# Routing attention and PReLU feed-forward: the keys' cluster masks four slots later on ScalarE, the range checks on inverted denominators

## The chip, the cores and the metric

The kernel runs on one core of one Trainium2 chip. The metric is the device time of one execution in microseconds; a comparison uses the median of several. The engines are named as the profile names them: PE is TensorE (PEld its weight loads), ACT is ScalarE, DVE is VectorE, POOL is GpSimd, SP is SyncE, which only issues transfers here. "L384" is line 384 of the kernel.

## The reference, cut to what matters

```python
# q, k, v: (4, 8, 768, 64), centroids: (8, 16, 64)
q_assign = argmax(einsum('bhsd,hcd->bhsc', q_n, c_n), -1)   # nearest of 16 clusters
k_assign = argmax(einsum('bhsd,hcd->bhsc', k_n, c_n), -1)
mask = q_assign[:, :, :, None] == k_assign[:, :, None, :]
scores = where(mask, q @ k^T / 8, -1e9)
attn = softmax(scores)                                       # minus the row's maximum
x = (attn @ v), heads joined: (3072, 512)
h = x @ w_in                                                 # w_in: (512, 2048), float64
g = maximum(h, 0) + alpha * minimum(h, 0)
out = g @ w_out                                              # w_out: (2048, 512), float64
```

The kernel leaves the row's maximum out of the softmax. So it checks that every denominator lay in a safe range, and has a general path behind one branch at its end for inputs where one did not.

## The kernel before

Work goes by pairs of heads (16 of them: 4 batches by 4), each in two halves of 384 queries, each half in three steps of two key chunks of 128. Pairs 0 to 3 (n < NCH) have their masks added to the scores by a small matmul; later pairs multiply the exponentials by the mask on VectorE. While the first pairs run, 32 tiles of float64 weights are fetched and turned into float32 in four stages: a fetch, a split on VectorE, a scaling on ScalarE, a joining on VectorE that ends with a multiplication on GpSimd.

A step has five slots. `tick` begins one and runs the pieces that `later` put off to it. Each engine executes its instructions in the order in which the program has them.

```python
ps_s = tile_pool(name="ps_s", bufs=2, space=PS)     # scores, two banks each
ps_v = tile_pool(name="ps_v", bufs=1, space=PS)     # product with v
ps_m = tile_pool(name="ps_m", bufs=1, space=PS)     # similarities, row sums and others
ps_f = tile_pool(name="ps_f", bufs=2, space=PS)     # feed-forward

def later(slots, piece):
    due.setdefault(now[0] + slots, []).append(piece)

def tick():
    now[0] += 1
    for piece in due.pop(now[0], []):
        piece()

# conversion of one weight tile, POOL's part last
def split():                                        # L241, L243, DVE
    nc.vector.tensor_scalar(out=power, in0=hi, scalar1=0x7FF00000, ...)
    nc.vector.tensor_scalar(out=dst.bitcast(U32), in0=hi, scalar1=0x000FFFFF, ...)
def scale():                                        # L247, L249, ACT
    nc.scalar.activation(out=power, in_=power, func=AF.Relu, ...)
    nc.scalar.activation(out=dst, in_=dst.bitcast(U32), func=AF.Identity, ...)
def join():                                         # L253, L256, DVE; L259, POOL
    nc.vector.scalar_tensor_tensor(out=power, in0=hi, ..., in1=power, ...)
    nc.vector.scalar_tensor_tensor(out=dst, in0=lo, ..., in1=dst, ...)
    nc.gpsimd.tensor_tensor(out=dst, in0=dst, in1=power.bitcast(FP32), op=ALU.mult)

def check(n, half, dens):                           # L310, two reductions
    i = 2 * n + half
    for to, op in ((lowest, ALU.min), (highest, ALU.max)):
        nc.vector.tensor_reduce(out=to[:, i:i + 1], in_=dens.bitcast(I32), axis=AX.X, op=op)

def prep_features(n, g):      # n < NCH: transposes L324 (PE), copies L328 (ACT) one slot later

def prep_sims(n):             # three steps ahead of pair n (n < NCH)
    ps = misc()
    ...                       # L351: similarities to the clusters, 8 matmuls
    later(1, lambda: prep_argmax(n, ps))

def prep_argmax(n, ps):
    ...                       # L359 to L377: argmax as one-hot rows, all DVE
    if n >= NCH:
        return                # (ahead of L377)
    member = fsp.tile([P, 2, HS], BF16, name="member")
    nc.vector.transpose(out=member[:, 0, :], in_=top...)          # L381
    for h in (1, 0):                                              # L384
        nc.scalar.activation(
            out=member[HP:P, h, :], in_=member[HP:P, 0, :], func=AF.Identity,
            scale=pick[HP:P, h:h + 1], bias=pick[HP:P, h + 2:h + 3])
    members[n] = member

def prep_queries(n, half, h): # L423, n < NCH: SP copies the query rows of member (partitions 0 to 63)

def score(n, half, chunks):
    ...                       # L463: scores; L473: adds the mask from member (n < NCH)
    ...                       # L484: exponentials, ACT, PSUM to SBUF

def invert(n, half):          # pairs 4 to 15: sums came by L530
    ps = totals.pop((n, half))
    inv = rdp.tile([P, 2 * NX], FP32, name="inv")
    nc.vector.reciprocal(out=inv, in_=ps[:, 0:2 * NX])            # L540
    check(n, half, ps[:, 0:2 * NX])
    ...                       # L545: two transposes spread inv into rd
    rds[n, half] = rd

def weigh(m, denominators=False):
    ...                       # L566: denominators by matmul (the early passes)
    ...                       # L573: product with v
    if denominators and done:
        ...                   # L579: transpose of the denominators out of PSUM
        check(n, half, denT[:, 0:NX // 2, 0])
        ...                   # L586, L590: reciprocals and copies to inv
        ...                   # L593: transpose to rd

def normalise(n, half):       # L600: xT = product * rd, DVE

# feed-forward of one half batch, in pieces between the steps:
#   hidden(f): L623 (PE), L630 and L631 (ACT), L615 (DVE); final(...): L643 (PE), L649 or L651

# one step of the first part:
tick(); score(step)
tick(); invert(prior); weigh(previous exponentials); mask, normalise(prior), add_up ...
for i in range(3):
    tick(); feed(...); prepare(...)      # prep_sims(n) in the first of these slots
    convert_next()                       # from step 1 on
```

The passes of pairs 0 to 3 in their first half are steps 0 to 11; their denominators come by L566. `invert` and L530 serve the 28 other passes.

Of the kernel before, what the change touches and what calls it, by code (L numbers as in the profile page):

```python
# [12 lines left out]
I32 = mybir.dt.int32  # L13
AF = mybir.ActivationFunctionType
ALU = mybir.AluOpType
AX = mybir.AxisListType
PS = bass.MemoryType.PSUM
P = 128
# [3 lines left out]
def kernel(  # L22
# [11 lines left out]
    nc = tc.nc  # L34
# [55 lines left out]
    def later(slots, piece):  # L90
        due.setdefault(now[0] + slots, []).append(piece)
# [57 lines left out]
    for g in range(P // Q):  # L149
        r = slice(g * Q, (g + 1) * Q)  # L150
        nc.gpsimd.tensor_copy(
            out=fold[r, :].rearrange("p (a i) -> p a i", i=Q),
            in_=ident[r, None, r].broadcast_to((Q, P // Q, Q)))
# [10 lines left out]
    pick = const.tile([P, 4], FP32, name="pick")  # L164
    for h in range(2):
        nc.vector.tensor_reduce(
            out=pick[:, h:h + 1],
            in_=fold.rearrange("p (a h c) -> p a h c", h=2, c=NC)[:, 0, h, :],
            axis=AX.X, op=ALU.add)
# [130 lines left out]

    lowest = const.tile([P, 2 * NP], FP32, name="lowest")
    highest = const.tile([P, 2 * NP], FP32, name="highest")
    WORDS = [float((127 + e) * 2 ** 23) for e in (-40, 50)]

    def check(n, half, dens):
        i = 2 * n + half
        for to, op in ((lowest, ALU.min), (highest, ALU.max)):
            nc.vector.tensor_reduce(out=to[:, i:i + 1], in_=dens.bitcast(I32), axis=AX.X,  # L310
                                    op=op)


# [28 lines left out]
    NX = GT * NG  # L342
    assert NB % NG == 0 and W == Q and GT == HJ and NX * Q == HS
    everys, keys, members = {}, {}, {}
    HP = P // 2

    def prep_sims(n):
        hp = pairs[n][1]
        ps = misc()
        for g in range(NG):  # L350
            nc.tensor.matmul(out=ps[g * W:(g + 1) * W, 0:HS],  # L351
                             lhsT=cT[:, hp * W:(hp + 1) * W],
                             rhs=qkTs[n][:, g * HS:(g + 1) * HS],
                             start=True, stop=True)
        later(1, lambda: prep_argmax(n, ps))

    def prep_argmax(n, ps):
        simT = asg.tile([P, HS], FP32, name="simT")
        nc.vector.transpose(out=simT, in_=ps[:, 0:HS])  # L359
        sim = simT.rearrange("p (t c) -> p t c", c=NC)  # L360


        mx = asg.tile([P, 2 * NX], FP32, name="mx")
        nc.vector.tensor_reduce(out=mx, in_=sim, axis=AX.X, op=ALU.max)
        top = asg.tile([P, 2 * NX, NC], BF16, name="top")
        nc.vector.tensor_tensor(
            out=top, in0=sim, in1=mx[:, :, None].broadcast_to((P, 2 * NX, NC)),
            op=ALU.is_ge)
        nc.vector.tensor_tensor(
            out=top, in0=top, in1=rank[:, None, :].broadcast_to((P, 2 * NX, NC)),  # L370
            op=ALU.mult)
        first = asg.tile([P, 2 * NX], BF16, name="first")
        nc.vector.tensor_reduce(out=first, in_=top, axis=AX.X, op=ALU.max)
        firsts[n] = first
        if n >= NCH:
            return
        nc.vector.tensor_tensor(  # L377
            out=top, in0=top, in1=first[:, :, None].broadcast_to((P, 2 * NX, NC)),
            op=ALU.is_equal)
        member = fsp.tile([P, 2, HS], BF16, name="member")  # L380
        nc.vector.transpose(out=member[:, 0, :], in_=top.rearrange("p t c -> p (t c)"))  # L381

        for h in (1, 0):
            nc.scalar.activation(  # L384
                out=member[HP:P, h, :], in_=member[HP:P, 0, :], func=AF.Identity,
                scale=pick[HP:P, h:h + 1], bias=pick[HP:P, h + 2:h + 3])
        members[n] = member

    def prep_clusters(n):


        first = firsts.pop(n)
        ps = misc()
        for g in range(NG):
            nc.tensor.matmul(out=ps[:, g * 2 * NX:(g + 1) * 2 * NX], lhsT=spread[:, g, :],
                             rhs=first, start=True, stop=True)
        every = fsp.tile([P, NG, GT, NG, 2], BF16, name="every")
        everys[n] = every
        later(1, lambda: nc.scalar.copy(every.rearrange("p g i r h -> p (g i r h)"),
                                        ps[:, 0:NG * 2 * NX]))  # L400
        later(2, lambda: prep_keys(n))
# [132 lines left out]
    def invert(n, half):  # L534

        if (n, half) not in totals:
            return
        ps = totals.pop((n, half))
        inv = rdp.tile([P, 2 * NX], FP32, name="inv")
        nc.vector.reciprocal(out=inv, in_=ps[:, 0:2 * NX])  # L540
        check(n, half, ps[:, 0:2 * NX])
        rd = rdp.tile([P, HS], FP32, name="rd")
        for h in range(2):
            r = slice(h * D, (h + 1) * D)
            nc.vector.transpose(  # L545
                out=rd[r, :],
                in_=inv[r, h * NX:(h + 1) * NX, None].broadcast_to((D, NX, Q)))
        rds[n, half] = rd

    def weigh(m, denominators=False):  # L550


        first = waiting[:m]
        del waiting[:m]
        n, half = first[0][:2]
        done = first[-1][2] == NJ - 1
        if (n, half) not in pos:
            pos[n, half] = ps_v.tile([P, 512], FP32, name="vps")
        po = pos[n, half]
        if denominators:  # L560

            for _, _, c, e in first:
                for h in range(2):
                    for x in range(2):
                        r = h * D + x * Q
                        nc.tensor.matmul(out=first_den[r:r + Q, 0:HS // 2],  # L566
                                         lhsT=ones[:, 0:Q],
                                         rhs=e[:, h, x * HS // 2:(x + 1) * HS // 2],
                                         start=(c == 0), stop=(c == NJ - 1))
        for _, _, c, e in first:  # L570
            for h in range(2):
                r = h * D
                nc.tensor.matmul(out=po[r:r + D, 0:HS], lhsT=vts[n][:, h, c, :],  # L573
                                 rhs=e[:, h, :], start=(c == 0), stop=(c == NJ - 1))
        if denominators and done:


            denT = asg.tile([P, NX, Q], FP32, name="simT")
            nc.vector.transpose(  # L579
                out=denT[:, 0:NX // 2, :].rearrange("p x i -> p (x i)"),  # L580
                in_=first_den[:, 0:HS // 2])
            check(n, half, denT[:, 0:NX // 2, 0])
            inv = rdp.tile([P, 2 * NX], FP32, name="inv")
            for g in range(P // Q):
                h, x = divmod(g, 2)
                nc.vector.reciprocal(  # L586
                    out=inv[h * D:h * D + Q, x * NX // 2:(x + 1) * NX // 2],
                    in_=denT[g * Q:(g + 1) * Q, 0:NX // 2, 0])
            for h in range(2):
                nc.vector.tensor_copy(out=inv[h * D + Q:(h + 1) * D, 0:NX],  # L590
                                      in_=inv[h * D:h * D + Q, 0:NX])
            rd = rdp.tile([P, HS], FP32, name="rd")
            nc.vector.transpose(out=rd, in_=inv[:, 0:NX, None].broadcast_to((P, NX, Q)))  # L593
            rds[n, half] = rd

    def normalise(n, half):
        b, hp = pairs[n]
        if (b, half) not in xTs:
            xTs[b, half] = xpool.tile([P, NCH, HS], FP32, name="xT")
        nc.vector.tensor_tensor(out=xTs[b, half][:, hp, :],  # L600
                                in0=pos.pop((n, half))[:, 0:HS],
                                in1=rds.pop((n, half)), op=ALU.mult)
# [114 lines left out]
    for u in range(-AHEAD, TOGETHER):  # L717
        for piece in load_at.get(u, []):
            piece()
        n, half, s = steps[max(u, 0)]  # L720
# [8 lines left out]
        if ended:  # L729
            invert(*prior[:2])  # L730
        if u > 0:
            weigh(GROUP, denominators=u <= UB)
# [33 lines left out]
    for u in range(TOGETHER, NS + 1):  # L766
        for piece in load_at.get(u, []):
            piece()
        if u < NS:
            n, half, s = steps[u]  # L770
        if s == 0 or u == NS:
# [3 lines left out]
            if u < NS:  # L775
                score(n, half, range(0, NJ // 2), alone=NJ // 2 - 1)
            tick()
            invert(*prior)
            weigh(GROUP if u == TOGETHER else NJ)
            if u < NS:  # L780
                for chunk in last(NJ // 2):
# [36 lines left out]
    while due:  # L818
# [3 lines left out]
    nc.vector.tensor_reduce(out=good[:, 1:2], in_=lowest, axis=AX.X, op=ALU.min)  # L822
    nc.vector.tensor_scalar(out=good[:, 0:1], in0=good[:, 0:1], scalar1=WORDS[1],
                            scalar2=None, op0=ALU.is_le)
    nc.vector.tensor_scalar(out=good[:, 1:2], in0=good[:, 1:2], scalar1=WORDS[0],
                            scalar2=good[:, 0:1], op0=ALU.is_ge, op1=ALU.mult)
# [163 lines left out]
```

## Time and profile before

| | |
|---|---|
| median of 3 runs | 1032.72 us (1032.67 to 1032.76) |
| span of the profiled execution | 1032.8 us |
| PE busy | 998.5 us, 97% |
| PEld busy | 490.1 us, 47% |
| DVE busy | 673.8 us, 65% |
| ACT busy | 325.0 us, 31% |
| POOL busy | 52.5 us, 5% |
| L384, masks on ACT | 8 instructions, 700 ns each, 14.6 to 68.0 us |
| L310, checks on DVE, pairs by L540 | 56 instructions, 168 and 121 ns each |
| L310, checks on DVE, beside L579 | 8 instructions, 163 and 152 ns each |
| ACT waited for L381 | 19.7 us in 4 times |
| PE's L351 waited for L310 | 4.1 us in 2 times |

Busy times are sums over the whole span. Their shares differ by stage: the first 97 us hold the early passes and most of the weights' conversion, then attention and feed-forward share TensorE, and the last 90 us are feed-forward alone. A line of waits reads: the waiting engine, tile and line, an arrow to what released it, the total in us, how many times, and the longest. Durations of neighbouring VectorE instructions can overlap in the trace, so the cost of a short one in a row is the distance between starts.

### The profile page before, as it was taken

What the parts mean: (1) busy time and instruction counts of PE and PEld (TensorE: products, weight loads), DVE (VectorE), ACT (ScalarE), POOL (GpSimd) and SP (SyncE); (2) the same over time, 40 slices, a digit from 0 to 9 for tenths busy, and PEclk for the clock granted to TensorE, in tenths of its full rate; (3) what the DMA queues carried; (4) which work ended last, traced back from release to release, by engine and by line L of the source; (5) the groups of instructions that cost most, each with busy time, mean ns of one, the idle gap of its engine ahead of it and who ended that gap; (6) DMA issues with size and microseconds to landing.
All of it is one profiled execution on the core that took longest, in us unless ns stands there. A gap on an engine that the chain in (4) does not pass through costs nothing.

```text
span 1032.8 us, 10335 instructions
## 1 busy us (share of the span) xinstructions
PE 998.5 (97%) x3923; PEld 490.1 (47%) x3923; DVE 673.8 (65%) x1183; ACT 325.0 (31%) x620; POOL 52.5 (5%) x71
## 2 busy tenths in 40 slices
PE   7789999899999999999999999999999999999997
PEld 4334444345454454545455454545545454544553
DVE  3688878868666576868856675878867675662111
ACT  3555545232232232313233141313324141321120
POOL 1132322200000000000000000000000000000000
PEclk8899999999999999999999999999999999999999
DMA  9343664121000230213000202304000000000000
GB/s 206 122 130 105 137 142 126 26 41 36 1 0 11 52 47 11 35 36 57 1 0 1 62 17 29 46 11 82 1 1 1 31 0 1 1 11 20 1 0 34
DMA packets 121705, 43.13 MB, mean 42 GB/s; under 512 B 113952, under 2 KB 114480, under 8 KB 121648
## 3 DMA queue, kind: packets, MB, share of 16 engines
q1 hardware_dynamic: 121472, 42.35, 18.7%
q8 instruction: 33, 0.54, 0.2%
q14 instruction: 24, 0.20, 0.1%
q10 hardware_dynamic: 176, 0.04, 0.0%
HBM read 35.69 MB, written 6.29 MB: 41 GB/s over the span
## 4 chain that ended last, share of the span: by engine, by line
PE 87%; DVE 8%; ACT 2%; issue 1%; POOL 1%; DVEq 0%; POOLq 0%
PE fps L623 31%; PE fps L643 30%; PE vps L573 11%; PE sps L463 9%; PE fps L463 3%; PE mps L351 1%; DVE power L253 1%; DVE acc L508 1%; PE sps L473 1%; DVE w_out_sb L243 1%; ACT member L384 1%; DVE w_in_sb L256 1%; DVE power L241 0%; PE fps L324 0%; DVE w_out_sb L256 0%
## 5 line engine op out<-in xcount | busy, mean ns | idle before, releaser
L623 PE MATMUL fps<-xT,w_in_sb 128*128 128x384 f32 x1024 | 342.6, 492 | 2.1 <-DVE xT L600 2.1
L643 PE MATMUL fps<-w_out_sb,gT 128*128 128x512 f32 x768 | 335.6, 594 | 0.9 <-DVE gT L615 0.9
L623 PEld LDWEIGHTS fps<-xT,w_in_sb 128*128 128x128 f32 x1024 | 192.1, 191 | 146.7 <-issue 7.8
L643 PEld LDWEIGHTS fps<-w_out_sb,gT 128*128 128x128 f32 x768 | 144.7, 190 | 177.8 <-issue 167.4
L615 DVE SCALAR_TENSOR_TENSOR gT<-neg,alpha_neg,gT 128x384 f32<-128x384 f32 x128 | 78.3, 613 | 132.7 <-ACT neg L631 131.3
L630 ACT ACTIVATE gT<-fps 128x384 f32<-128x384 f32 x128 | 62.7, 490 | 276.7 <-PE fps L623 276.7
L463 PE MATMUL sps<-qkT 64*128 64x384 f32 x576 | 115.2, 520 | 10.3 <-ACT E L484 10.3
L497 DVE SCALAR_TENSOR_TENSOR raw<-aq,key,raw 128x384 f32<-128x384 bf16 x160 | 88.8, 614 | 19.4 <-ACT raw L481 11.1
L484 ACT ACTIVATE E<-sps 128x768 f32<-128x768 f32 x88 | 67.2, 813 | 68.7 <-PE sps L473 42.6
L573 PE MATMUL vps<-E,vt 128*64 128x384 f32 x448 | 82.0, 493 | 0.0
L497 DVE SCALAR_TENSOR_TENSOR E<-aq,key,E 128x384 f32<-128x384 bf16 x128 | 71.3, 613 | 11.9 <-ACT E L484 6.2
L463 PEld LDWEIGHTS sps<-qkT 64*128 64x128 f32 x576 | 53.5, 193 | 52.3 <-ACT E L484 16.1
L508 DVE TENSOR_TENSOR acc<-acc,E 128x768 f32<-128x768 f32 x64 | 66.4, 1038 | 8.3 <-ACT E L484 6.5
L651 DVE TENSOR_TENSOR y<-y,fps 128x512 f32<-128x512 f32 x30 | 20.5, 685 | 67.2 <-PE fps L643 67.2
L631 ACT ACTIVATE neg<-fps 128x384 f32<-128x384 f32 x128 | 62.1, 485 | 0.0
L484 ACT ACTIVATE raw<-sps 128x768 f32<-128x768 f32 x56 | 42.9, 814 | 52.6 <-PE sps L463 51.9
L573 PE MATMUL vps<-raw,vt 128*64 128x384 f32 x320 | 56.5, 491 | 0.0
L649 ACT COPY y<-fps 128x512 f32<-128x512 f32 x24 | 14.0, 585 | 130.0 <-PE fps L643 130.0
L573 PEld LDWEIGHTS vps<-E,vt 128*64 128x64 f32 x448 | 29.3, 136 | 40.7 <-issue 39.8
L508 DVE TENSOR_TENSOR acc<-acc,raw 128x768 f32<-128x768 f32 x48 | 45.9, 956 | 1.1
L463 PE MATMUL fps<-qkT 64*128 64x384 f32 x192 | 41.5, 508 | 0.0
L481 ACT ACTIVATE raw<-fps 128x384 f32<-128x384 f32 x48 | 21.0, 494 | 59.2 <-PE fps L463 59.2
(100 smaller groups left out, 613.4 us busy)
## 6 DMA issues: line engine op xcount, KB each, us to landing
raw<-in_moe_w_in_dram SPq DMA_DIRECT2D x16, 512.0 KB, 4.3
raw<-in_moe_w_out_dram SPq DMA_DIRECT2D x16, 512.0 KB, 3.7
vt<-in_v_dram SPq DMA_DIRECT2D x16, 384.0 KB, 4.2
out_dram<-y SPq DMA_DIRECT2D x24, 256.0 KB, 2.0
qk<-in_q_dram SPq DMA_DIRECT2D x48, 96.0 KB, 4.0
qk<-in_k_dram SPq DMA_DIRECT2D x48, 96.0 KB, 3.5
qk<-in_q_dram SPq DMA_DIRECT2D x8, 192.0 KB, 4.5
qk<-in_k_dram SPq DMA_DIRECT2D x8, 192.0 KB, 4.5
```

The costliest lines, as they stand in the source:

```text
L463: nc.tensor.matmul(out=bank(ps, h), lhsT=qkT[r:r + D, S + c * P:S + (c + 1) * P], rhs=qkT[r:r + D, half * HS:(half + 1) * HS], start=True, ...
L481: nc.scalar.activation(out=E[:, h, :], in_=ps[h][:, 0:HS], func=AF.Exp, scale=SCALE)
L484: nc.scalar.activation(out=E, in_=ps[:, :, 0:HS], func=AF.Exp, scale=SCALE)
L497: nc.vector.scalar_tensor_tensor(out=E[:, h, :], in0=aqs[n, half][:, h, :], scalar=keys[n][:, NJ + c, h:h + 1], in1=E[:, h, :], op0=ALU.is ...
L508: nc.vector.tensor_tensor(out=acc, in0=acc if first is None else first[3], in1=E, op=ALU.add)
L573: nc.tensor.matmul(out=po[r:r + D, 0:HS], lhsT=vts[n][:, h, c, :], rhs=e[:, h, :], start=(c == 0), stop=(c == NJ - 1))
L615: nc.vector.scalar_tensor_tensor(out=gs[f], in0=neg, scalar=alpha_neg[:, f:f + 1], in1=gs[f], op0=ALU.mult, op1=ALU.add)
L623: nc.tensor.matmul(out=ps[:, 0:HS], lhsT=w_in_sb[:, c, f * P:(f + 1) * P], rhs=xT[:, c, :], start=(c == 0), stop=(c == NCH - 1))
L630: nc.scalar.activation(out=gs[f], in_=ps[:, 0:HS], func=AF.Relu)
L631: nc.scalar.activation(out=neg, in_=ps[:, 0:HS], func=AF.Relu, scale=-1.0)
L643: nc.tensor.matmul(out=ps[:, 0:DM], lhsT=gs[f][:, i * P:(i + 1) * P], rhs=w_out_sb[:, f, :], start=on and f == f0, stop=off and f == f0 + ...
L651: nc.vector.tensor_tensor(out=ys[i], in0=ys[i], in1=ps[:, 0:DM], op=ALU.add)
```

## The change

It has two parts. The two ScalarE instructions that make the keys' half of a pair's mask from the one-hot rows leave `prep_argmax` and are put four slots later, so that ScalarE comes to them when VectorE has had time for the argmax. And the range check reads the inverted denominators in SBUF in place of the denominators, with the range inverted too (2^-50 to 2^40 instead of 2^-40 to 2^50); it stands behind the transposes that spread the inverses, or one slot later, so that the PSUM bank of the row sums is read by the reciprocal alone. The number of instructions stays.

```diff
-    WORDS = [float((127 + e) * 2 ** 23) for e in (-40, 50)]
-    def check(n, half, dens):
+    WORDS = [float((127 + e) * 2 ** 23) for e in (-50, 40)]
+    def check(n, half, inverses):
 ...
-            nc.vector.tensor_reduce(out=to[:, i:i + 1], in_=dens.bitcast(I32), axis=AX.X,
+            nc.vector.tensor_reduce(out=to[:, i:i + 1], in_=inverses.bitcast(I32), axis=AX.X,
 ...  (prep_argmax)
-        for h in (1, 0):
-            nc.scalar.activation(
-                out=member[HP:P, h, :], in_=member[HP:P, 0, :], func=AF.Identity,
-                scale=pick[HP:P, h:h + 1], bias=pick[HP:P, h + 2:h + 3])
+        def of_heads():
+            for h in (1, 0):
+                nc.scalar.activation(
+                    out=member[HP:P, h, :], in_=member[HP:P, 0, :], func=AF.Identity,
+                    scale=pick[HP:P, h:h + 1], bias=pick[HP:P, h + 2:h + 3])
+
         members[n] = member
+        later(4, of_heads)
 ...  (invert)
         nc.vector.reciprocal(out=inv, in_=ps[:, 0:2 * NX])
-        check(n, half, ps[:, 0:2 * NX])
 ...
         rds[n, half] = rd
+        check(n, half, inv)
 ...  (weigh)
-            check(n, half, denT[:, 0:NX // 2, 0])
 ...
             rds[n, half] = rd
+            later(1, lambda: check(n, half, inv[:, 0:NX]))
```

## The prediction, made before the changed kernel had run

> **What bounds the kernel now.** I read the page's busy shares first (TensorE busy 97% of the span), then the table of stretches, because a share over the whole span hides that the stages have different limits. In it the columns are the stretch, its length, busy time of PE, PEld, DVE, ACT and POOL (with instruction counts), the granted TensorE clock, and the DMA share and rate.
>
> ```profile
> 26.80:39.60 12.80, 10.33 (x80) 4.75 (x80) 4.41 (x9) 8.06 (x13) 1.38 (x1) 0.87 0.46 168
> 39.60:97.00 57.40, 47.10 (x366) 19.30 (x364) 51.12 (x107) 32.30 (x51) 17.43 (x12) 0.94 0.38 123
> 97.00:142.00 45.00, 44.91 (x164) 21.53 (x164) 33.78 (x57) 25.18 (x45) 12.10 (x8) 0.96 0.52 123
> 142.00:250.00 108.00, 100.78 (x397) 46.89 (x396) 87.59 (x149) 38.21 (x71) 16.86 (x11) 1.00 0.33 70
> 250.00:1032.00 782.00, 775.86 (x2811) 386.72 (x2809) 487.19 (x838) 211.97 (x428) 0.00 (x0) 1.00 0.10 20
> ```
>
> After 250 us TensorE idles 6.1 us of 782, so nothing that only shortens waits can bring much there. The masks that the change moves are made for the first four head pairs alone, between 14 and 68 us. The change must earn its time before 97 us, where TensorE idles 2.5 + 10.3 us after 26.8, and a shift won there has to survive to the end.
>
> The waits (who waited <- for whom: total us, times, longest) between 26 and 98 us:
>
> ```profile
> ...
> ACT member L384 <- DVE member L381: 13.9, 3, 5.0
> PE sps L463 <- ACT E L484: 10.3, 3, 4.0
> ...
> DVE power L241 <- DMA raw<-in_moe_w_in_dram: 5.0, 1, 5.0
> DVE power L253 <- ACT power L247: 4.8, 5, 1.8
> ...
> DVE simT L579 <- PE fps L566: 3.3, 2, 1.7
> ...
> PE fps L623 <- DVE xT L600: 2.1, 1, 2.1
> ```
>
> Lines one and two are one story. ScalarE stands at the mask for VectorE's argmax; the exponentials behind it in its queue, whose scores are long in PSUM, stand with it; the next scores find no free bank, so TensorE stands too. The chain of waits (start, duration, what) shows the second occurrence:
>
> ```profile
> 45.85 0.59 DVE member L381
> 46.47 0.71 ACT member L384
> 47.20 0.70 ACT member L384
> 47.92 0.72 ACT power L247
> 48.64 0.52 ACT w_in_sb L249
> 49.16 0.70 ACT E L484
> 49.91 2.93 PE sps L463 x8
> ```
>
> The last line also shows a clock lost: eight score matmuls in 2.93 us, where the same eight take 1.49 us at 57.57.
>
> **What the Trainium skill says.** "PSUM — Partial Sum Buffer", section "Engine vs sequencer instructions": ScalarE's and VectorE's queues are strictly first in, first out. The seven lines above agree: exponentials of finished scores wait behind a mask. "TensorE: Matmul & The Clock Gate", section "What's actually happening": after an idle window of about 3.4 us the clock falls to half until activity returns. Here the granted clock is 0.53 in 49.9 to 53.3 us, after 4.0 us idle. "SBUF — State Buffer", section "Who interferes with whom": VectorE in a two-port mode, or with two SBUF inputs, and GpSimd take turns on a shared port pair, and the loser blocks for the whole instruction. The trace agrees: the conversion's L243 takes 0.42 us alone and 1.50 us where GpSimd's L259 (1.38 us) runs. Most of my estimate hangs on this third one.
>
> **The change part by part.**
>
> 1. *Masks four slots later.* Nothing is added or removed: eight 0.70 us instructions stay. A step has five slots. For pairs 1, 2 and 3 they fall behind the next step's exponentials. For pair 0 nothing else lies between on ScalarE, so its 5.9 us wait at the start, with TensorE's 3.9 us for L328, stays.
>
> TensorE's own account would be 2.23 + 4.03 + 4.05 us of waiting plus the cold matmuls (2.82 + 2.93 + 2.93 instead of three times 1.49: 4.2 us; the small ones after them about 0.7): 15 us. **That is the ceiling, not the gain**, because from 39.6 us the feature stage hands over to VectorE: 51.1 us busy of 57.4, and without a gap on the chain from 79 us to the last xT at 96.4, for which TensorE waits at 97. So I replay VectorE's order with TensorE and ScalarE earlier, using the durations of the trace.
>
> First pair. TensorE is through with the product at 26.84 and need not wait. Scores of step 2 take 1.49 + 0.43 (L463, L473) and end at 28.76; denominators and product of the step before take 0.83 + 1.44, the next pair's transposes and key copies 1.92 (34.87 to 36.79 in the chain), scores of step 3 again 1.92, denominators 0.83: these are ready at 35.7 instead of 39.55. VectorE's second conversion starts at 32.34 in both cases (it waits for its DMA, issued at 27.93 behind the query-mask DMA, which follows the unchanged argmax). Its next wait, 1.84 us for ScalarE's L247, goes: L247 now starts near 30.4. VectorE so reaches L579 at 38.00 - 1.84 = 36.16 instead of 39.57. **Gain 3.41 us**: 1.84 plus the 1.57 waited for the denominators.
>
> Second pair. VectorE runs unbroken through inversion and argmax. Its short waits for ScalarE at 48.67 (0.39) and 55.61 (1.16) look reclaimable, but GpSimd's L259 runs at 48.36 to 49.63 and 53.81 to 55.59: the next two-input instruction would stop at the port pair instead, and end at the same moment. I count both as zero. The wait of 1.70 us before L579 at 60.34 is for TensorE. For TensorE, 35.70 + 1.44 (product) + 0.79 (L351) + 1.92 (scores 4) + 0.83 + 1.44 puts scores of step 5 at 42.1 instead of 49.9. They end at 44.0, but ScalarE first has the moved mask of pair 2 (behind the argmax, which ends at 46.43 - 3.41 = 43.0; 1.43 us) and a conversion (1.34 us), so their exponentials run from 45.8 to 47.3. Its next conversion needs VectorE's L243, done at 52.53 - 3.41 = 49.1, and takes 1.34 us; key copies and the transposes between them take 1.25 us (56.25 to 57.50 before), scores 1.92, denominators 0.83: ready at 54.5. VectorE arrives at 58.64 - 3.41 = 55.23. So the 1.70 goes whole. **Sum 5.11 us.**
>
> Third pair and on. L579 at 79.22 had no wait; the 0.40 at 69.46 and 1.04 at 76.25 again coincide with L259 (69.14 to 70.41, 74.58 to 76.34). From there to xT VectorE has no gaps. TensorE's third wait (4.05 us) is therefore worth nothing: TensorE reaches the feed-forward earlier and waits longer for xT there. Its clock is cold there now already (0.56 in 97.05 to 100.5), so that penalty stays.
>
> 2. *Checks in the first four pairs* leave the way to xT. The chain shows L310 at 39.99 and the reciprocal at 40.22, but the starts are 39.99 and 40.14: two checks cost 0.15 us of VectorE there. Twice as many columns in the new place (12 for 6) hardly matter, and they run after the last xT. **Sum 5.26 us.**
>
> 3. *Checks in the other 28 inversions* are not removed; starts at 161.63 and 161.75 put the pair at 0.12 us. Behind the transposes they free the bank by that much sooner. Only TensorE's L351 at 161.89 and 194.75 waited for it (1.1 and 3.0 us), and almost all of that was for VectorE arriving at L540. From 142 to 195 us the chain is VectorE's, so only the second counts: 0.12 us. The transposes and xT come 0.12 us sooner each time, where nothing waits. **Sum 5.4 us.**
>
> Carrying it on: 97 to 142 us is TensorE without idle, 142 to 195 VectorE, the rest TensorE; all start from xT, and no transfer there is tied to absolute time, since the fetches wait for the tiles that VectorE frees. So 5.4 us stay: 1032.7 - 5.4 = 1027.3 us.
>
> **The rivals.**
>
> *A: the ceiling.* If TensorE bounded all of the first 97 us, 10.3 us of waits and 4.9 us of cold clock go: 1017.5 us. For it speaks the chain, which runs through all three waits. Against it: VectorE's 51.1 of 57.4 us, and its gapless run from 79 to 96.9, which TensorE's earlier start can't shorten.
>
> *B: hidden anyway.* If VectorE bounded the stage from the first conversion on, only the 0.15 would stay: 1032.5 us. Against it are the 1.84, 1.57 and 1.70 us during which VectorE idled with GpSimd idle too.
>
> *C: a new wait.* The moved masks again stand in front of exponentials, one step later: if the argmax is not done by then, the wait only moves. In my replay the mask of pair 2 starts when its argmax ends, near 43.0, and the exponentials behind it are due only at 44.0, so it costs little; ScalarE's conversion after it costs more. Should the conversions' order hold TensorE back a further 1 to 2 us before L579 at 60, about 1029 us.
>
> *D: the port pair gives way.* If VectorE does use the short waits that I set to zero (0.39 + 1.16 + 0.40 + 1.04 = 3.0 us), about 1024.3 us; if TensorE, less idle in one piece before 97, is warm there, up to 1.7 us more.
>
> **Range and chances.** The estimate is 1027.3 us. C and D give the range: 1024.3 to 1029.6 us. Two per cent is 20.7 us, more than the ceiling of A, and nothing in the change adds work, so within 2% is nearly certain.
>
> **What would show it.** Right: ScalarE's wait for L381 falls from 19.7 us to little over the first 5.9; TensorE's wait for L484 (10.3) goes almost whole; its wait for L600 at the first feed-forward grows from 2.1 to several us; L579 first starts near 36.2 and the second near 55.2; L623 runs on from about 91.8; VectorE's busy time stays near 674 us. Wrong: L579 late in the second pair with TensorE waiting for key copies (C); VectorE's L253 starting without a stretched duration next to L259 (D); or shifts of the first 97 us that shrink before 250, which would mean a time-bound transfer or a wait that I did not see in the stretch from 142 to 195.

## The result, and the profile after

The changed kernel took 1027.09 us (median of 4 runs, 1024.60 to 1030.15), the kernel before 1032.74 us beside it. The ratio is 0.9943, with a 95% interval of 0.9915 to 0.9972. The prediction was 1027.3 us.

In the profile after, the line numbers have moved: L310 is now L311, L324 is L325, L328 is L329, L351 is L352, L381 is L382, L384 is L386, L463 is L467, L473 is L477, L484 is L488, L540 is L544, L566 is L570, L573 is L577, L579 is L583, L600 is L604, L623 is L627 and L643 is L647. First the table of stretches, with the columns as before; the second stretch ends where the feed-forward starts.

```profile
26.80:39.60 12.80, 12.56 (x106) 5.60 (x104) 7.48 (x21) 9.52 (x15) 1.39 (x1) 1.00 0.49 169
39.60:91.80 52.20, 44.93 (x342) 18.90 (x341) 49.55 (x93) 29.90 (x45) 17.86 (x12) 0.90 0.41 135
91.80:97.00 5.20, 5.20 (x18) 2.97 (x16) 2.95 (x9) 4.00 (x8) 0.00 (x0) 1.00 0.00 0
```

TensorE now fills the first of these stretches almost wholly (12.56 of 12.80 us instead of 10.33), but from 39.6 us on it still idles 7.3 of 52.2 us. VectorE is the one nearly without gaps there: 49.6 of 52.2 us. Its one long wait, 1.16 us at 80.69, is for GpSimd's L259. The waits of the changed kernel between 26 and 98 us say what TensorE waits for now:

```profile
...
ACT member L386 <- DVE member L382: 3.3, 3, 1.5
PE fps L325 <- ACT qkT L329: 3.0, 2, 2.8
ACT power L247 <- DVE power L241: 2.9, 4, 1.2
...
PE fps L570 <- DVE simT L583: 2.5, 1, 2.5
...
PE fps L627 <- DVE xT L604: 1.1, 1, 1.1
PE vps L577 <- DVE xT L604: 1.0, 1, 1.0
...
DVE simT L583 <- PE fps L570: 0.2, 1, 0.2
```

TensorE's wait for the exponentials (10.3 us before) is gone from the list. ScalarE's wait for the last step of the argmax (L382) fell from 13.9 to 3.3 us in this stretch. Ahead of xT of the fourth pair, VectorE's waits for TensorE and ScalarE (L579 and L253, 3.3 and 4.8 us before) are down to 0.2. In their place TensorE waits for VectorE, also in the middle of the stage (L570, L577), and ScalarE's conversion waits for VectorE's split. The timeline of ScalarE (start, duration, instruction, and in brackets the idle time ahead of it with its releaser) shows the new order where the second mask falls:

```profile
39.84 1.51 ACT L488 ACTIVATE E<-sps 128x768 f32<-128x768 f32 x2 [1.23 <-PE sps L477]
42.88 1.43 ACT L386 ACTIVATE member<-member,pick 64x384 bf16<-64x384 bf16 x2 [1.53 <-DVE member L382]
44.34 0.72 ACT L247 ACTIVATE power<-power,low_exp 128x512 uint32<-128x512 uint32 x1
44.97 0.61 ACT L249 ACTIVATE w_in_sb<-w_in_sb 128x512 f32<-128x512 uint32 x1
45.49 1.49 ACT L488 ACTIVATE E<-sps 128x768 f32<-128x768 f32 x2
```

The exponentials of step 4 run at 39.84, ahead of the mask; in the kernel before they came after it (49.16 in its chain). The mask still waits 1.5 us, and the next exponentials stand behind it and a conversion until 45.5, about as the replay had it (45.8).

### The profile page after: what moved, and what is told of

It is laid out like the page before. It is cut to its first block, busy times and chain, and to the rows that moved or that the text cites. A ratio compares the mean times of both kernels' runs of the same rounds, so it can differ in the third digit from the quotient of the medians.

```text
span 1025.3 us, 10333 instructions
## 1 busy us (share of the span) xinstructions
PE 996.5 (97%) x3923; PEld 489.3 (48%) x3923; DVE 678.6 (66%) x1183; ACT 325.5 (32%) x620; POOL 53.0 (5%) x71
## 4 chain that ended last, share of the span: by engine, by line
PE 86%; DVE 9%; issue 1%; POOL 1%; DMA 1%; ACT 1%; SPq 1%; DVEq 0%; POOLq 0%
PE fps L627 31%; PE fps L647 30%; PE vps L577 10%; PE sps L467 8%; PE fps L467 3%; DVE power L253 1%; PE mps L352 1%; DVE w_in_sb L243 1%; DVE w_in_sb L256 1%; DVE power L241 1%; DVE w_out_sb L256 1%; DVE acc L512 1%; DVE w_out_sb L243 1%; POOL w_in_sb L259 0%; SPq L119 0%
## 5 line engine op out<-in xcount | busy, mean ns | idle before, releaser
L627 PE MATMUL fps<-xT,w_in_sb 128*128 128x384 f32 x1024 | 341.0, 490 | 1.1 <-DVE xT L604 1.1
L647 PE MATMUL fps<-w_out_sb,gT 128*128 128x512 f32 x768 | 335.6, 594 | 0.9 <-DVE gT L619 0.9
L627 PEld LDWEIGHTS fps<-xT,w_in_sb 128*128 128x128 f32 x1024 | 191.2, 190 | 145.0 <-issue 5.3
L647 PEld LDWEIGHTS fps<-w_out_sb,gT 128*128 128x128 f32 x768 | 144.7, 190 | 177.8 <-issue 167.4
L467 PE MATMUL sps<-qkT 64*128 64x384 f32 x576 | 113.0, 512 | 0.0
L488 ACT ACTIVATE E<-sps 128x768 f32<-128x768 f32 x88 | 67.1, 812 | 68.4 <-PE sps L477 42.3
L577 PE MATMUL vps<-E,vt 128*64 128x384 f32 x448 | 83.3, 500 | 1.0 <-DVE xT L604 1.0
L467 PEld LDWEIGHTS sps<-qkT 64*128 64x128 f32 x576 | 52.9, 191 | 42.3 <-issue 9.3
L488 ACT ACTIVATE raw<-sps 128x768 f32<-128x768 f32 x56 | 42.9, 814 | 52.6 <-PE sps L467 51.9
L577 PE MATMUL vps<-raw,vt 128*64 128x384 f32 x320 | 56.5, 491 | 0.0
L577 PEld LDWEIGHTS vps<-E,vt 128*64 128x64 f32 x448 | 29.6, 138 | 42.5 <-issue 40.5
L467 PE MATMUL fps<-qkT 64*128 64x384 f32 x192 | 41.4, 508 | 0.0
```

The source lines that it names most:

```text
L467: nc.tensor.matmul(out=bank(ps, h), lhsT=qkT[r:r + D, S + c * P:S + (c + 1) * P], rhs=qkT[r:r + D, half * HS:(half + 1) * HS], start=True, ...
L488: nc.scalar.activation(out=E, in_=ps[:, :, 0:HS], func=AF.Exp, scale=SCALE)
L627: nc.tensor.matmul(out=ps[:, 0:HS], lhsT=w_in_sb[:, c, f * P:(f + 1) * P], rhs=xT[:, c, :], start=(c == 0), stop=(c == NCH - 1))
L647: nc.tensor.matmul(out=ps[:, 0:DM], lhsT=gs[f][:, i * P:(i + 1) * P], rhs=w_out_sb[:, f, :], start=on and f == f0, stop=off and f == f0 + ...
```

## The experiments

**Either part alone.** The masks alone, on the kernel before:

```diff
-        for h in (1, 0):
-            nc.scalar.activation(out=member[HP:P, h, :], ...)
+        def of_heads():
+            for h in (1, 0):
+                nc.scalar.activation(out=member[HP:P, h, :], ...)
+
         members[n] = member
+        later(4, of_heads)
```

> The masks four slots later, checks as in the kernel before. Theory: nearly the whole gain, 0.15 to 0.4 us less than the full change: 5 to 7 us below the kernel before, xT about 0.15 us later than in the changed kernel. Rival (the freed bank or the shorter way to xT carries the gain): at most half of it, 1030 us or more.

Measured: 1028.11 us (median of 6), ratio 0.9943 (0.9922 to 0.9964), 5.45 us below the kernel before beside it (1033.56) and the same ratio as the whole change. Its trace has xT of the fourth pair at 88.88 us, 1.75 us ahead of the changed kernel's 90.63, where I had expected it 0.15 us behind; the last section shows where this comes from. The checks alone, on the kernel before:

```diff
-        check(n, half, ps[:, 0:2 * NX])
+        check(n, half, inv)                                 # after rd
-            check(n, half, denT[:, 0:NX // 2, 0])
+            later(1, lambda: check(n, half, inv[:, 0:NX]))  # range inverted too
```

> The checks on the inverted denominators, masks as before. Theory: 0.1 to 0.5 us below the kernel before, 1032.3 us; TensorE's waits for L484 stay at 10.3 us. Rival (the bank carries the gain): 2 us or more below the kernel before, TensorE's wait for the similarities' bank (4.1 us) shrinking by as much.

Measured: 1033.40 us (median of 14), ratio 1.0001 (0.9990 to 1.0011); TensorE's waits for the exponentials stayed at 10.1 us, and its two waits for the similarities' bank went from 4.1 to 3.9 us. So the gain is that of the masks. What the checks save is to be seen only in a trace: from the start of the denominators' transpose to that of xT it is 2.44 us with the checks between (93.95 to 96.39 in the kernel before) and 2.30 us without (92.35 to 94.65 here).

**Where the mask stands.** Two slots instead of four:

```diff
-        later(4, of_heads)
+        later(2, of_heads)
```

> The changed kernel with the masks two slots behind the argmax instead of four: on ScalarE they are then still ahead of the next step's exponentials, as in the kernel before; the order on every other engine is that of the changed kernel. Theory (only the place relative to the exponentials counts): the gain is gone, 1032 to 1034 us, TensorE's three waits for L488 are back with about 10 us. Rival (VectorE needs only some slots' head start): half the gain or more, under 1030 us.

Measured: 1032.59 us (median of 12, 1028.88 to 1036.86), ratio 0.9996 (0.9980 to 1.0013). The first line of TensorE's waits in its trace:

```profile
PE sps L467 <- ACT E L488: 8.2, 3, 3.3
```

All three waits are back, and in the median the gain is gone. Two slots later ScalarE still reaches the mask ahead of the next step's exponentials:

```profile
44.45 1.43 ACT L386 ACTIVATE member<-member,pick 64x384 bf16<-64x384 bf16 x2 [3.90 <-DVE member L382]
45.90 1.51 ACT L488 ACTIVATE E<-sps 128x768 f32<-128x768 f32 x2
```

Yet the trace (an execution of 1031.63 us) does not show that half the head start is worth nothing. A conversion that stood between mask and exponentials before now goes ahead of the mask, the waits are shorter (8.2 us, not the 10 expected), and xT of the fourth pair starts at 91.94 us: 4.45 us ahead of the trace of the kernel before and 1.3 us behind the changed kernel. Behind xT it then loses 3.0 us against the changed kernel, by the clock: the 18 records of L627 take 7.73 us instead of 6.04, and eight of L647 5.40 us instead of 3.70. In this trace, then, the lost gain is not the order on ScalarE alone; how the two share it over all twelve executions stays open. Nine slots:

```diff
-        later(4, of_heads)
+        later(9, of_heads)
```

> The changed kernel with the masks nine slots behind: one step's exponentials and a conversion's scaling more pass ahead of them. Theory (past the exponentials VectorE bounds the stage, and TensorE's 2.8 us wait for the key copies is a wait for VectorE's L243 by way of ScalarE): xT of the fourth pair within 0.5 us of the changed kernel's 90.6 us, when the start of the first L583 is set equal; 1025 to 1029 us. Rival (the moved mask still holds the exponentials back, a new wait that the four slots leave): TensorE's wait for L329 goes, xT 1 to 3 us earlier.

Measured: 1029.23 us (median of 5), ratio 0.9954 (0.9935 to 0.9973), a little above the range I gave. In its trace xT of the fourth pair starts 54.34 us after the first L583, against 54.64 in the changed kernel, so more distance brings at most 0.3 us. TensorE's wait for L329 stayed (8.3 us with the one at the start, 7.3 in the changed kernel). A cost is new: pair 0's mask is late as well, TensorE's L477 waits 0.5 us for it, and L583 starts at 36.77 with 1.08 us of waiting ahead of it instead of at 35.99. In this trace, too, the eight L647 records near 189 us took 5.40 us.

**VectorE's own work, or the port pair.** The last multiplication of each weight tile moves from GpSimd to VectorE:

```diff
-            nc.gpsimd.tensor_tensor(out=dst, in0=dst, in1=power.bitcast(FP32), op=ALU.mult)
+            nc.vector.tensor_tensor(out=dst, in0=dst, in1=power.bitcast(FP32), op=ALU.mult)
```

> The changed kernel with the conversion's last multiplication on VectorE instead of GpSimd: VectorE gets 32 instructions of about 0.6 us more, 19 us in all, some 12 of them ahead of the first xT, and GpSimd touches no port in that stretch. Theory (from 39.6 us on VectorE bounds the stage, but through the port pair): L243 is never stretched to 1.5 us, xT comes 5 to 7 us earlier than in the changed kernel although VectorE does more, and the stretch from 142 to 195 us gains some more; 1014 to 1021 us. Rival (VectorE's own work bounds the stage, the coincidences with GpSimd mean nothing): xT about 7 us later, 1034 us or more.

Measured: 1024.90 us (median of 6), ratio 0.9921 (0.9904 to 0.9937), 1.9 us below the changed kernel beside it (1026.80): faster than the kernel before, but less than I expected. VectorE's L243 (busy time, mean ns of one), first in the changed kernel, then here:

```profile
L243 DVE TENSOR_SCALAR w_out_sb<-raw 128x512 uint32<-128x512 uint32 x16 | 12.1, 756 | 0.0
```

```profile
L243 DVE TENSOR_SCALAR w_out_sb<-raw 128x512 uint32<-128x512 uint32 x16 | 6.8, 423 | 0.0
```

L243 never stretches now (none of the 32 takes over 0.47 us). xT of the fourth pair starts at 85.40 instead of 90.63 us, though VectorE has 32 instructions of 0.69 us more in all. That is the shift expected (5 to 7 us), and it shows that up to there the changed kernel is bound by VectorE with its waits for GpSimd in it. Not all of them need be the port pair: the 1.16 us at 80.69, where L241 waits until an L259 is done, go with the move as well, and the run does not separate the two. The second half of the expectation failed: VectorE reaches the row sums' reciprocal L544 5.24 us earlier (181.66 instead of 186.90), the same shift as at xT, so 142 to 195 us gained nothing more. TensorE waits longer for that bank, 4.3 us instead of 2.9, and runs cold behind it: L352 and L647 take 1.51 and 5.41 us instead of 0.85 and 3.70, which loses 2.4 of the 5.2 us again.

**Fewer conversions ahead of that wait**, on the kernel with the multiplication on VectorE:

```diff
-        converting = 0 if u < 1 else 1 + (u % 3 == 2) if u < UB else 2
+        converting = 0 if u < 1 else 1 + (u % 3 == 2) if u < UB else 2 if u < UB + 6 else 1
```

> The last multiplication on VectorE, and from step 18 on one weight tile converted per step instead of two, so that some two conversions (2.6 us of VectorE each) move behind the row sums of the pass for which TensorE waits at 177 to 182 us. Theory (VectorE bounds the stretch from 142 to 195 us too, and a wait of 4.3 us throws TensorE into its cold clock): that wait shrinks to under 1.5 us, no cold window there, 1018 to 1022 us. Rival (TensorE gets no sooner to the end because the feed-forward then waits for its weights): a wait of L647 or L627 for VectorE of 3 us or more near 200 us, and 1024 us or more.

Measured: 1024.12 us (median of 6), ratio 0.9910 (0.9894 to 0.9927), above the range of my theory. The 4.3 us wait is gone (L352 starts at 178.78 without one, and L647 behind it takes 3.70 us), as the theory had it; the rival's new wait took its place, at 207.5 us:

```profile
PE fps L647 <- DVE w_out_sb L259: 3.1, 1, 3.1
```

**The TensorE clock.** The same program differs from execution to execution by up to 5.8 us. Two traces, of programs that differ in the checks alone, show one way in which this can come about. In both, TensorE waits 2.9 to 3.0 us for the row sums of the same pass. The changed kernel:

```profile
187.27 0.85 PE L352 MATMUL mps<-qkT,cT 128*32 128x384 f32 x8 [2.88 <-DVE inv L544]
188.05 3.70 PE L647 MATMUL fps<-w_out_sb,gT 128*128 128x512 f32 x8
```

The masks alone (its L351 and L646 are L352 and L647 here):

```profile
185.58 1.51 PE L351 MATMUL mps<-qkT,cT 128*32 128x384 f32 x8 [3.00 <-DVE highest L310]
187.02 6.05 PE L646 MATMUL fps<-w_out_sb,gT 128*128 128x512 f32 x8
```

The same sixteen matmul records take 7.5 us instead of 4.5, at a granted clock of 0.50 from 185.6 to 190.4 us (1.00 in the changed kernel). This alone undoes the 1.8 us by which that trace had reached xT earlier (88.88 against 90.63). The changed kernel was run twice more, for its spread:

> The changed kernel once more, for its spread. Theory (VectorE with the port pair bounds the stage up to xT, and the TensorE clock in single windows makes the spread): L583 first starts at 36.0 us and xT of the fourth pair near 90.6 us in this trace too; 1025 to 1029 us, and where the time differs from the profiled 1027.27 us, the difference lies in windows of cold clock (about 1.7 us each) where TensorE is the bound. Rival (the stage is bound by TensorE, and the 7.5 us of that one trace are its share): xT moves with the time of the run.

> The changed kernel once more, beside the next one. Its ten times so far lie in three groups, near 1024.5, 1026.9 and 1029.7 us. Theory (single windows of cold clock after waits that trip it in some executions only): the same three levels again. Rival (drift between chips or hours): one level.

Measured: 1026.80 us (ratio 0.9939, 0.9919 to 0.9960) and 1027.34 us (0.9949, 0.9934 to 0.9963), six runs each. With the first four that is sixteen times: four at 1029.4 us or more, two under 1025, ten between 1026.4 and 1028. The groups are less sharp than I expected, and the second repeat has no low one. The mean granted clock goes with them: 0.987 in each of the four, 0.994 in the two, 0.990 to 0.994 in the ten. The traced executions all come from the ten (1027.27, 1026.65 and 1027.23 us, xT of the fourth pair at 90.63, 90.23 and 90.40, L647 behind the wait at 3.70 us each time), so no trace shows where one of the four loses its time, and the rival of the first expectation stays untested. Then the idle 2.9 us were filled:

```diff
         hp = pairs[n][1]
+        if n == NCH + 1:
+            busy = ps_s.tile([P, 2, 512], FP32, name="sps")
+            for _ in range(4):
+                nc.tensor.matmul(out=busy[:, 0, 0:HS], lhsT=ident, rhs=qkTs[n][:, 0:HS],
+                                 start=True, stop=True)
         ps = misc()
```

> The changed kernel with four matmuls that nobody reads (2.7 us) ahead of the similarities of pair 5, where TensorE idles 2.9 us. Theory (the group near 1029.7 us is that wait tripping the cold clock): no time above 1028 us, the lowest still near 1024.5 us. Rival (the wait has no part in the spread): times near 1029.7 us in about three of ten.

Measured: 1026.24 us (median of 6, 1025.29 to 1027.14), ratio 0.9937 (0.9924 to 0.9949). No time lies near 1029.7; the lowest is not near 1024.5 either. Six runs could miss a group of one in four by chance (0.75 to the sixth is 0.18), so the times alone don't settle it. The same with six matmuls on the kernel with the multiplication on VectorE, where the wait is 4.3 us:

```diff
+        if n == NCH + 1:
+            ...                       # as above, range(6)
```

> The last multiplication on VectorE, and six matmuls that nobody reads (4.0 us) put ahead of the similarities of pair 5, where TensorE otherwise idles 4.3 us; they write a score bank that is free then. Theory (idle time costs again afterwards, by the cold clock): the similarities start as before, but the stretch behind them runs warm: about 1.7 us less than with the multiplication on VectorE alone, 1022 to 1024 us. Rival (the clock has no part in the time): equal or later, 1025 us or more.

Measured: 1022.72 us (median of 5, 1021.66 to 1024.25), ratio 0.9899 (0.9882 to 0.9917). Behind the wait the eight L647 records (line 652 there) take 3.70 us instead of 5.41 us, and L352 0.85 instead of 1.51. Matmuls that nobody reads took away these 2.4 us; the ratios (0.9899 and 0.9921, each to the kernel before beside it) say about 2 us, though their intervals overlap a little.

**The start.** Five more of them where TensorE waits 3.9 us for the first key copies:

```diff
+        if (n, g) == (1, 2):                  # in prep_features
+            busy = ps_s.tile([P, 2, 512], FP32, name="sps")
+            for _ in range(5):
+                nc.tensor.matmul(out=busy[:, 0, 0:HS], lhsT=ident, rhs=qkTs[0][:, 0:HS],
+                                 start=True, stop=True)
```

> The last multiplication on VectorE, the six unread matmuls ahead of pair 5's similarities, and five more (3.4 us) into the 3.9 us that TensorE idles at the start, behind which the first scores run at half clock (2.93 us for eight matmuls instead of 1.49). Theory (the start is bound by TensorE up to the second argmax, so the cold clock there costs in full): scores of step 0 take 1.5 us, everything behind shifts by 1.5 to 2.3 us, 1020 to 1021.5 us. Rival (the start is bound by transfers): 1022.7 us as without them; or the five matmuls themselves run cold and push the start back by up to 3 us.

Measured: 1021.34 us (median of 4, 1020.19 to 1021.72), ratio 0.9884 (0.9867 to 0.9901). The timeline of TensorE in the changed kernel, then here (line 477 here is L467, line 487 is L477):

```profile
17.68 2.93 PE L467 MATMUL sps<-qkT 64*128 64x384 f32 x8
```

```profile
17.22 1.56 PE L477 MATMUL sps<-qkT 64*128 64x384 f32 x8
19.43 0.69 PE L487 MATMUL sps<-aq,member 32*128 32x384 bf16 x4 [0.65 <-DMA aq<-member]
```

The scores run warm, and 0.65 us of the saving goes to a new wait, for the transfer of the query masks. The first transpose of the denominators comes 1.55 us sooner than without the five (34.01 against 35.56). But the lead shrinks: at xT of the fourth pair it is 0.74 us (84.79 against 85.53), at the row sums 0.41 us (181.41 against 181.82), and the two traced executions took 1021.58 and 1021.66 us. So the traces do not show that the 1.4 us between the medians are the start's. This version, with the multiplication on VectorE and both fillings, beats the kernel before and the changed kernel (1027.34 us beside it). All its outputs are computed as in the changed kernel; the eleven extra matmuls are read by nobody.

## Why the prediction was right, step by step

- *First pair.* L579 was put at 36.16 us instead of 39.57; as L583 it started at 35.99. Both of VectorE's waits, 1.84 and 1.57 us, went whole, as that trace had them (see *Partly luck*).
- *Second pair.* Put at 55.23, it started at 54.87. The margin was thin: VectorE waited 0.23 us for TensorE's denominators, which I had ready 0.7 us sooner than VectorE. TensorE lost 2.77 us at the key copies and ran cold behind it (2.62 us for eight score matmuls), which the replay did not have. Of the short waits beside GpSimd that I set to zero, a few tenths came back: from the first L583 to the second it took 18.88 with that 0.23 in it, where my replay had 19.07, and from the second to the third 18.58 instead of 18.88. Rival D was right by that much, 0.7 us of its 3.0.
- *Third pair and on.* xT of the fourth pair was put at 91.13 and started at 90.63; the feed-forward ran on from 91.33, put at 91.8. The 15 us of TensorE's own account stayed a ceiling.
- *The checks.* 0.15 us was the estimate for the first four pairs, and the traces show 0.14. In the other inversions they save nothing that the times show.
- *Carrying it on.* From xT of the fourth pair (L604 or L600) to the end of the span it was 934.7 us after and 936.4 before. The difference is the clock of the 18 matmul records behind that xT, before and after:

```profile
97.09 7.74 PE L623 MATMUL fps<-xT,w_in_sb 128*128 128x384 f32 x18 [2.07 <-DVE xT L600]
91.33 6.04 PE L627 MATMUL fps<-xT,w_in_sb 128*128 128x384 f32 x18 [1.07 <-DVE xT L604]
```

My step "that penalty stays" was wrong: all three traces of the changed kernel have 6.04 us here. The other traces bear the reading out. Where neither this window nor the one behind the row sums is cold, it is 934.6 to 934.7 us from that xT to the end (three traces of the changed kernel, one of it with the idle 2.9 us filled); with one of them cold, by 1.7 us, 936.1 to 936.4 (the kernel before, the checks alone, nine slots); with both (two slots) or with the long one of 3.0 us (the masks alone) 937.7. The two profiled spans differ by 7.5 us (1032.8 and 1025.3), the medians by 5.65: the profiled execution of the kernel before took 1034.77 us, 2 us over its median.
- *Partly luck.* That execution gave the replay its durations. In it the scores behind TensorE's first wait ran cold (2.82 us), so that L247 came late and VectorE waited 1.84 us for it. In the trace of the checks alone, where the masks stand as before (1032.93 us, near its median), the same scores took 1.62 us, VectorE waited 0.21 us, the first L579 started at 37.67 instead of 39.57 and xT of the fourth pair at 94.65 instead of 96.39. The changed kernel, which differs from it in the masks alone, is 4.0 us ahead of that at xT, where my sum had 5.11, and gains 1.6 us more behind xT, where I had nothing. Measured from that execution, one term of my sum was too large, then, and the clock behind xT was missing; the two errors nearly cancel. These are single traces: how often the first scores run cold is not known. And an agreement of 0.2 us in the medians is far finer than the scatter below.
- *Wrong in what to look for.* I expected TensorE to wait several us for xT at the first feed-forward. It waited 1.1 us, because VectorE had already held it up at L570 and L577 (2.5 and 1.0 us): an engine ahead of its supplier meets it at the first shared buffer, not only at the last. ScalarE's wait for L382 came to 9.2 us over the whole span, not to little over 5.9. And VectorE's busy time rose from 673.8 to 678.6 us with the same instructions. L241, L243 and L256 are stretched more often beside GpSimd (3.1 us more together; a mean of 753 instead of 720 ns for L256, 449 instead of 419 for L241), L253 less (1.7 us), and the checks take 1.5 us more.
- *The median hides a scatter* that I had not counted. The prediction's range took in the port pair and the conversions; the executions themselves spread over 5.8 us (1024.35 to 1030.15 in sixteen), a little past the range's upper end.

## What to carry to other kernels

Put an instruction that waits for another engine behind those that are ready on its own in-order queue; here four slots put it there, nine brought no more, and with two, ahead of them, the median stayed that of the kernel before. Before you add up the waits that this removes, replay the engine that will be the bound next, with the durations of a trace whose time is near the median, and count little of a short wait of it where a shared port is held meanwhile (here about 0.7 us of 3.0 came back). Where TensorE can't be kept supplied for 2 to 4 us (the waits that did this here), the idle time may be paid a second time by the clock behind it; with a wait of 4.3 us, filling it with matmuls that nobody reads took away 2.4 us.

## What the runs showed of the hardware

Two waits of 2.9 and 3.0 us at the same place differed in what followed: one left the clock at 1.00, one halved it for over 5 us. Shorter ones halved it too: 2.07 us ahead of L623 in the kernel before (0.56 in the 3.4 us behind it), 2.23 us ahead of its scores at 29.07 (0.52), 2.45 us ahead of L570 in the changed kernel (0.50, sixteen records in 1.51 us instead of 0.86). So the idle window of about 3.4 us that the prediction quotes was no lower bound for a wait here, as far as the profile can tell when TensorE is idle. The Trainium skill's page "TensorE: Matmul & The Clock Gate", section "What's actually happening", says that the activity is judged in windows that run freely, not from the start of the kernel; that would make the outcome a matter of phase. The runs fit this, but no run here shows the phase itself. Nor was it tried to take away the waits at L325 and L570 one by one, so which windows make the low group of times stays open, and whether it is the clock alone.

Which of VectorE and GpSimd waits for the other can tip between programs that do the same there: L243 ahead of the second L583 took 1.50 to 1.52 us in the three traces of the changed kernel, beside an L259 of 1.39 us in the first, and 0.44 us in that of the masks alone, where L259 took 1.76 us instead. It tipped the same way with the idle 2.9 us filled (0.43 and 1.75 us). The starts of the two, counted from the L256 ahead of them, agree within 0.02 us with those in the first trace of the changed kernel, so what tips it is not shown. Its worth is: from the first to the second transpose of the denominators it is 17.5 us in these two traces instead of 18.6 to 18.9, and xT of the fourth pair comes 1.4 to 2.0 us sooner. This is a second source of scatter beside the clock.
